# Attention and a two-layer network on one core: keys and queries split at full height, a third form of the products with the values, and neighbouring 64-row products

## The chip, the core and the metric

The kernel runs on one core of a Trainium2 chip. The metric is the time of one launch on the device, in microseconds (us). A core has TensorE (matrix products; PE in the profile, with its weight loads as PEld), VectorE (DVE), ScalarE (ACT), GpSimd (POOL), and SyncE (SP), which issues nearly all transfers here. Each works through its own queue in the order in which the program was written, and they wait for each other on semaphores.

## The reference

```python
batch, n_heads, seq, head_dim = 4, 12, 448, 64
scores = matmul(q, k.T) / sqrt(64)
scores = cap * tanh(scores / cap)              # cap = 30
attn = softmax(scores)                         # over the keys
x = matmul(attn, v)                            # heads side by side: [1792, 768]
h = x @ w_in                                   # [768, 2048]
out = maximum(0.01 * h, h) @ w_out             # [2048, 768]
```

All of it is fp32. A second path, for a cap above 40, stands behind the program's end and isn't taken.

## The kernel before

**Precision.** TensorE has a rounded fp32 form (fp32r here) that takes one pass for a product and a whole one that takes four. Nearly every operand is therefore kept as two parts: `hi`, a copy rounded to fp32r, and `lo`, the remainder. A product is then three passes: hi by hi, hi by lo, lo by hi (line 712). `split` (line 343) makes the parts: a copy on ScalarE or VectorE, then a subtraction on VectorE or GpSimd.

**Attention** goes by pairs of heads, 24 in all (six for each of four batches). Two heads have 896 keys, which are seven tiles of 128: three that belong to the first head (A0 to A2), three to the second (B1 to B3), and one, M, with the last 64 keys of the first head and the first 64 of the second. For a pair, SyncE loads k, q and v; VectorE transposes k and q into `kT` and `qT`, 128 rows of which 64 belong to each head. `stack` (line 449) then builds `kst0` and `kst1`, one for each head: on the head's own 64 rows the hi part of its keys, on the other 64 rows the remainder, so that one pass computes two of the three products. For each head it does a 64-row copy from `kT` and a 64-row subtraction, and a 64 by 64 corner for M into `kb`. Queries are split at 128 rows into `qn` and `qlo` (line 499) and copied, 64 rows at a time, into `qd` and `qz` by an engine or by a transfer. Scores (line 563) take 15 passes a pair and go to PSUM; ScalarE applies tanh (line 575) and exp (line 577) and writes the exponentials `pf`, as keys by queries.

**Products with the values** come in two forms. Pairs 0 to 13 multiply `pf` by the values in whole fp32 (line 591), with a column of ones beside the values, which gives the sums. Pairs 14 to 23 split `pf` into `ph` and `pl` and have the values' hi and lo parts side by side in the weights, so that two passes suffice (lines 434 and 435); the sums are made apart, by adding on VectorE and GpSimd. In both forms head 0's result goes to `po0` and head 1's to `po1`, in different banks of PSUM. For tile M each head uses its own 64 rows alone; head 0 has M last, head 1 has it first or last, and the steps of the two heads are independent of each other.

**The network** runs as 34 units a batch (136 in all): 16 of the first layer (18 passes) and 18 of the second (15 or 18 passes), all at line 687, fed by weights that are split into `w` again for every batch. The result of a unit leaves PSUM through ScalarE (line 722) and VectorE (lines 727 and 736).

**Order.** `Plan` collects steps with a rank and a cost for each engine that could do them. `issue` is a list scheduler: it repeatedly takes the step that can start first by those costs (and by rank among equals), gives it to the engine that would end it first, and writes the instruction there. So the costs and ranks, the table `T` among them, set the order of every queue; SyncE's queue is one of them.

Of the kernel before, what the change touches and what calls it, by code (L numbers as in the profile page):

```python
# [21 lines left out]
    kT=1,  # L22
# [25 lines left out]
    role={'x fixed_vx': -279.8, 'x fixed_v': -32.4, 'pair kraw dma first': -114.6, 'pair kT first': -66.5, 'pair qT first': 8.1, 'pair kst first': 606.4, 'pair kb first': 43.4, 'pair qn first': 404.6, 'pair qlo first': 17.3, 'pair qd first': -209.0, 'pair vx dma first': -44.3, 'pair po first': -143.3, 'pair sums first': 20.8, 'pair rt first': -18.8, 'pair xh first': 234.6, 'pair xl first': -9.0, 'pair vhi first': 5.3, 'pair vlo first': -10.0, 'pair ph first': 8.5, 'pair kraw dma': -80.3, 'pair kT': -351.0, 'pair qraw dma': 216.2, 'pair qT': 158.0, 'pair kst': 58.5, 'pair qn': 715.7, 'pair qlo': 177.0, 'pair vraw dma': 1208.5, 'pair vhi': -301.0, 'pair vlo': -249.7, 'pair ph': -297.4, 'pair pl': 272.8, 'pair po': 65.9, 'pair x': -133.1, 'pair xh': 602.7, 'pair xl': -26.0, 'unit wr dma first': -298.3, 'unit wm first': 89.1, 'unit ws first': -117.6, 'unit scratch dma first': -7.5, 'unit whi first': 97.6, 'unit wlo first': -164.9, 'unit m first': 339.7, 'unit a first': 108.0, 'unit g first': -626.7, 'unit gh first': -746.5, 'unit gl first': -737.6, 'unit acc first': -52.0, 'unit ot first': 88.7, 'unit store dma first': -7.8, 'unit ws dma': 11.8, 'unit whi': 244.8, 'unit wlo': -45.3, 'unit m': 176.3, 'unit a': -38.5, 'unit g': -828.4, 'unit gh': 775.4, 'unit acc': -397.5, 'unit ot': -15.1, 'unit store dma': -171.8, 'unit kraw': 2.4, 'unit qraw': 20.2, 'x cap dma': -698.3, 'x inv': -321.8, 'x ones': -257.6, 'pair qraw dma first': -47.2, 'pair pl first': -5.5, 'pair kb': 777.6, 'pair qd': -145.0, 'pair sc': -71.0, 'pair pf': -287.8, 'pair sums': -262.3, 'pair rt': -218.0, 'pair t': -278.4, 'pair u': -779.0, 'pair uh': -90.3, 'pair ul': 95.2, 'pair ss': -59.8, 'unit gl': -222.5, 'pair vhi.0 zero': 4.1, 'pair vlo.0 zero': -2.7, 'pair ph.0 zero': 2.7, 'pair ph.1 zero': 2.7, 'pair ph.2 zero': 2.7, 'pair ph.3 zero': 2.7, 'pair pl.0 zero': -5.3, 'pair pl.1 zero': -5.3, 'pair pl.2 zero': -5.3, 'pair pl.3 zero': -5.3, 'pair pf first': -131.6, 'pair k0.0 dma zero': 83.1, 'pair q0.0 dma zero': 88.5, 'pair kT0.0 zero': 138.8, 'pair kst0.0 zero': -36.0, 'pair kb.0 zero': 66.5, 'pair qd.0 zero': 8.2, 'pair qlo0.0 zero': -72.2, 'pair q0.1 zero': 10.7, 'pair k0.1 dma zero': 29.5, 'pair q0.1 dma zero': 111.6, 'pair kT0.1 zero': -24.2, 'pair qT0.1 zero': -55.6, 'pair kst1.0 zero': 38.4, 'pair qlo0.1 zero': -12.5, 'pair vx.0 dma zero': -19.5, 'pair sc.0 zero': 3.1, 'pair sc.1 zero': -33.6, 'pair pf.1 zero': 84.1, 'pair pf.2 zero': 587.4, 'pair sc.3 zero': -33.0, 'pair pf.3 zero': -20.3, 'pair po0.0 zero': -1.7, 'pair x.0 zero': 68.1, 'pair po1.0 zero': 28.6, 'pair rt.0 zero': -28.3, 'pair sums.1 zero': -12.7, 'pair x.1 zero': -19.7, 'pair xl.0 zero': -29.3, 'pair sc first': -150.8, 'pair x first': 13.6, 'pair xs': 138.0, 'pair q0.0 zero': 16.0, 'pair qT0.0 zero': -25.2, 'pair qd.1 zero': 79.5, 'pair sc.2 zero': 182.8, 'pair xh.0 zero': 30.1, 'pair pf.0 zero': 4.5, 'pair vhi dma': 26.6, 'pair vx dma': 4.5, 'unit raw first': 36.6},  # L48
    pair=[-1101.8, -433.2, -1118.2, -327.2, 39.0, 378.0, 325.9, 703.0, 321.7, 372.6, 475.8, 149.5, 521.9, 787.1, 552.8, 471.0, 783.4, 77.4, 446.9, 129.6, 408.3, 288.7, 835.1, 264.8],
# [15 lines left out]


class Plan:

    LAT = {"dma": 2.2}

    def __init__(self):
        self.steps = []  # L80
        self.rings = {}
        self.slots = {}
        self.kind, self.phase, self.shift = "x", "", 0.0

    def part(self, kind, phase, shift):

        self.kind, self.phase, self.shift = kind, phase, shift

    def ring(self, tag, n):
# [9 lines left out]
    def add(self, rank, cost, fn, reads=(), writes=(), after=(), lat=0.15, freed=(), port=True):  # L99
        tag = writes[0][0].rstrip("0123456789") if writes else "store"  # L100
        if self.phase == " zero":
            tag = f"{writes[0][0]}.{writes[0][1]}"
        role = self.kind + " " + tag + (" dma" if list(cost) == ["sp"] else "") + self.phase
        rank = hundredths(rank) + hundredths(self.shift) + hundredths(T["role"].get(role, 0.0))
        self.steps.append(dict(role=role, rank=rank, cost={e: hundredths(c) for e, c in cost.items()}, fn=fn, reads=reads,
                               writes=writes, after=list(after), lat=hundredths(lat), freed=freed, port=port))
        return len(self.steps) - 1

# [784 lines left out]
```

## Time and profile before

| | us |
|---|---|
| three runs | 757.99, 758.2, 759.87 |
| median | 758.2 |
| the profiled execution, its whole time | 758.92 |
| its span, first to last instruction | 757.1 |
| TensorE busy in the span | 701.7 |
| VectorE busy | 572.8 |
| ScalarE busy | 512.3 |
| GpSimd busy | 135.7 |

The profile is of one execution, so sums are made against its span of 757.1 us. The mean granted clock of TensorE was 0.977. A row of a matmul runs from the start of a pass to the end of its modelled pipeline, so neighbouring rows overlap: the start-to-start distance is what a pass costs in a dense stream. A whole fp32 product is recorded as two rows. A few rows are missing from the trace.

### The profile page before, as it was taken

The page shows a single profiled execution, that of the slowest core. Times are in us where ns is not written, and L with a number is a line of the kernel's source. Part 1 is how long each engine was busy: PE and PEld are TensorE (multiplying, and loading weights), DVE is VectorE, ACT ScalarE, POOL GpSimd, SP SyncE. Part 2 cuts the span into 40 slices and gives each one's busy share as a digit, 9 for nine tenths or more (in the row PEclk, how much of TensorE's full clock was granted, in tenths as well). Part 3 has the DMA queues.
Part 4 walks back from the last instruction along what each step waited for, and adds up shares of the span by engine and source line. Part 5 has one row for each costly group of instructions (what it writes and reads, how often), then busy time and mean ns, then how long its engine had stood idle before and what let it go on. Part 6 is the DMA issues. An engine that isn't in the chain of part 4 may idle for free.

```text
span 757.1 us, 9414 instructions
## 1 busy us (share of the span) xinstructions
PE 701.7 (93%) x3084; PEld 573.7 (76%) x3084; DVE 572.8 (76%) x856; ACT 512.3 (68%) x778; POOL 135.7 (18%) x132
## 2 busy tenths in 40 slices
PE   7897999999988989899999999999899988999994
PEld 4453578777667777788888888988778876999884
DVE  7888788779878788987799787786986986435443
ACT  6877797788978777885687557666965963434230
POOL 2332320010112111110033211221231420000000
PEclk9998999999999999999999999999999998999997
DMA  6887764976787677635254365443233362333335
GB/s 118 178 198 201 172 169 144 259 229 149 219 226 186 211 206 167 138 94 140 58 140 117 98 137 133 122 113 109 58 97 109 72 144 66 113 105 96 95 92 86
DMA packets 206215, 105.33 MB, mean 139 GB/s; under 512 B 160432, under 2 KB 188720, under 8 KB 206160
## 3 DMA queue, kind: packets, MB, share of 16 engines
q1 hardware_dynamic: 206096, 104.55, 54.1%
q8 instruction: 26, 0.43, 0.3%
q14 instruction: 29, 0.24, 0.1%
q0 software_dynamic: 64, 0.11, 0.1%
HBM read 79.89 MB, written 18.09 MB: 129 GB/s over the span
## 4 chain that ended last, share of the span: by engine, by line
PE 63%; DVE 17%; ACT 9%; DMA 6%; issue 4%; SPq 1%; DVEq 0%; ACTq 0%
PE m L687 48%; PE po L591 6%; PE sc L563 5%; PE po L434 2%; DVE w L238 2%; DMA wr<-in_moe_w_in_dram 2%; PE po L435 2%; ACT pf L575 1%; DVE kst L238 1%; DVE ws L679 1%; DVE wr L676 1%; DVE late L727 1%; DVE pl L238 1%; ACT pf L577 1%; DMA qraw<-in_q_dram 1%
## 5 line engine op out<-in xcount | busy, mean ns | idle before, releaser
L687 PE MATMUL m<-gh,w 128*128 128x448 f32 x768 | 236.1, 375 | 6.7 <-DVE late L736 3.8
L687 PE MATMUL m<-xh,w 128*128 128x448 f32 x768 | 232.7, 374 | 10.2 <-DVE late L727 7.3
L687 PEld LDWEIGHTS m<-xh,w 128*128 128x128 f32 x768 | 145.7, 190 | 30.0 <-DVE late L727 10.5
L687 PEld LDWEIGHTS m<-gh,w 128*128 128x128 f32 x768 | 145.9, 190 | 27.5 <-DVE late L736 4.6
L238 DVE TENSOR_TENSOR w<-ws,w 128x768 fp32r<-128x768 f32 (+1 forms) x124 | 118.5, 963 | 38.4 <-ACT w L231 36.5
L687 PE MATMUL m<-xl,w 128*128 128x448 f32 x384 | 141.9, 370 | 0.2 <-DVE xl L238 0.2
L687 PE MATMUL m<-gl,w 128*128 128x448 f32 x384 | 141.9, 370 | 0.0
L231 ACT CAST w<-ws 128x768 fp32r<-128x768 f32 (+1 forms) x110 | 86.2, 788 | 60.1 <-PE m L687 26.0
L575 ACT ACTIVATE pf<-sc,inv_sb 128x896 f32<-128x896 f32 (+1 forms) x82 | 74.2, 913 | 22.2 <-PE sc L563 11.2
L563 PE MATMUL sc<-qd,kst 128*128 128x448 f32 x192 | 73.4, 402 | 12.2 <-ACT pf L575 8.2
L687 PEld LDWEIGHTS m<-gl,w 128*128 128x128 f32 x384 | 73.1, 190 | 7.1 <-issue 1.1
L687 PEld LDWEIGHTS m<-xl,w 128*128 128x128 f32 x384 | 73.0, 190 | 7.1 <-issue 0.7
L577 ACT ACTIVATE pf<-pf,cap_sb 128x896 f32<-128x896 f32 (+1 forms) x82 | 77.6, 952 | 0.7
L591 PE MATMUL po<-pf,v 128*128 128x448 f32 (+1 forms) x170 | 69.0, 569 | 5.8 <-ACT w L231 2.3
L722 ACT ACTIVATE late<-m 128x448 f32<-128x448 f32 x58 | 31.4, 542 | 53.6 <-PE m L687 50.9
L727 DVE TENSOR_TENSOR late<-m,late 128x448 f32<-128x448 f32 x64 | 39.6, 619 | 28.6 <-ACT late L722 28.3
L563 PEld LDWEIGHTS sc<-qd,kst 128*128 128x128 f32 x192 | 35.9, 188 | 27.7 <-ACT pf L575 14.3
L563 PE MATMUL sc<-qz,kst 128*128 128x448 f32 x144 | 52.7, 366 | 0.2 <-ACT qz L231 0.2
L591 PEld LDWEIGHTS po<-pf,v 128*128 128x128 f32 (+1 forms) x170 | 27.3, 191 | 32.3 <-issue 20.5
L238 POOL TENSOR_TENSOR w<-ws,w 128x640 fp32r<-128x640 f32 (+1 forms) x12 | 21.9, 1830 | 151.4 <-PE m L687 113.0
L736 DVE TENSOR_TENSOR late<-m,late 128x448 f32<-128x448 f32 x48 | 29.4, 617 | 24.5 <-PE m L687 24.1
L238 DVE TENSOR_TENSOR gl<-late,gh 128x448 fp32r<-128x448 f32 x62 | 40.7, 659 | 6.6 <-ACT gh L231 5.9
(110 smaller groups left out, 954.4 us busy)
## 6 DMA issues: line engine op xcount, KB each, us to landing
ws<-scratch SPq DMA_DIRECT2D x66, 384.0 KB, 3.2
wr<-in_moe_w_in_dram SPq DMA_DIRECT2D x16, 768.0 KB, 5.4
ws<-scratch SPq DMA_DIRECT2D x36, 320.0 KB, 2.9
scratch<-ws SPq DMA_DIRECT2D x22, 384.0 KB, 5.5
wr<-in_moe_w_out_dram SPq DMA_DIRECT2D x12, 640.0 KB, 5.0
kraw<-in_k_dram SPq DMA_DIRECT2D x96, 56.0 KB, 2.4
qraw<-in_q_dram SPq DMA_DIRECT2D x94, 56.0 KB, 2.7
wr<-in_moe_w_out_dram SPq DMA_DIRECT2D x6, 768.0 KB, 5.1
```

The lines of the kernel that those rows point to most:

```text
L231: nc.scalar.copy(o, i)
L238: ENG[eng].tensor_tensor(out=o, in0=a, in1=f32(b), op=ALU.subtract)
L434: nc.tensor.matmul(at(f"po{j}", i)[:, 0:S], v_, at("ph", ver)[k, t], start=(m == 0), stop=False)
L435: nc.tensor.matmul(at(f"po{j}", i)[:, 0:S], v_, at("pl", ver)[k, t], start=False, stop=(m == 3))
L563: nc.tensor.matmul(at("sc", ver)[:, t, 0:S], l, r, start=(m == 0), stop=(m == len(mm) - 1))
L575: a = plan.add(r, {"act": ct}, lambda e, sc=sc, pf=pf: nc.scalar.activation(pf(), sc(), AF.Tanh, scale=inv_sb), [("sc", ver), ("inv", 0)], ...
L577: plan.add(r, {"act": ct + 0.03}, lambda e, pf=pf: nc.scalar.activation(pf(), pf(), AF.Exp, scale=cap_sb), (), [("pf", ver)], after=[a])
L591: nc.tensor.matmul(at(f"po{j}", i)[:, 0:S], at("vx", i)[k, c, j:j + 2].rearrange("p o d -> p (o d)"), at("pf", ver)[k, t], start=(n == 0), ...
L687: nc.tensor.matmul(o, l, r, start=(first and m == 0), stop=(last and m == len(mm) - 1))
L722: nc.scalar.mul(at("a", f), ps(), 0.01)
L727: plan.add(rank, {"dve": 0.54}, lambda e: nc.vector.tensor_tensor(out=at("g", f), in0=ps(), in1=at("a", f), op=ALU.max), [("m", m), ("a", ...
L736: op = plan.add(rank, {"dve": 0.54}, lambda e: nc.vector.tensor_tensor(out=acc(), in0=ps(), in1=acc(), op=ALU.add), [("m", m)], [(tag, b)] ...
```

## The change

1. **Third form of the products ("parts").** Pairs 10 to 13 now split `pf` and the values, and do hi by `ph`, hi by `pl` and lo by `ph`. The values' tile has six columns of 64 a chunk: hi of head 0, a fixed one, hi of head 1, lo of head 0, a fixed zero, lo of head 1. So the sums come with the products as in the whole form. Pairs 0 to 9 stay whole.
2. **M's products in one step.** `products` replaces both old loops. The step `shared` does tile M for both heads, one pass of head 0 and one of head 1 in turn.
3. **Keys and queries.** `kT` is copied whole into `kh` and the remainder is written over `kT` (as `kl`). The 64-row halves of both go to `kst0` and `kst1` by `put`: ScalarE, VectorE, GpSimd, or a transfer on SyncE's queue. The corners of `kb` may go by transfer too. `kh` and `kT` have one buffer; `qd`, once a ring of three, is one buffer for each head.
4. **The leak of the first layer** is written into `g`, which becomes a ring of three; the buffer `a` is gone.
5. **Costs, delays and ranks.** The scheduler's costs are new (a pass 0.2045 instead of 0.19), a step's result is taken to be ready 0.10 to 0.20 us after it, with 0.20 more on the way to TensorE, and all ranks in `T` are new. Pair 0 keeps its own code.

```diff
+    np=10,
...
-    LAT = {"dma": 2.2}
+    LAT = {"act": 13, "dve": 12, "pool": 10, "pe": 20}
...
-                lat = max(220, s["lat"]) if eng == "sp" else 0 if eng == "pe" and "pe" in steps[u]["cost"] else s["lat"]
+                to_pe = "pe" in steps[u]["cost"]
+                lat = max(220, s["lat"]) if eng == "sp" else 0 if eng == "pe" and to_pe else self.LAT[eng]
+                lat += 20 if to_pe and eng != "pe" else 0
...
-    ring("qd", T["qd"], [P, S], F32R)
+    ring("kh", 1, [P, S])
+    plan.ring("kl", 1)
+    for j in range(2):
+        ring(f"qd{j}", 1, [P, S], F32R)
...
-    MM = 0.19
-    HALF = {"act": 0.47, "dve": 0.30, "pool": 1.09}
+    MM = 0.2045
+    HALF = {"act": 0.575, "dve": 0.40, "pool": 1.1}
+    MOVE = dict(HALF, sp=0.48)
...
+    way = lambda i: "whole" if i < T["np"] else "parts" if i < SUMS else "sums"
+    def products(i, r0, where):
...
+        def passes(j, c, k, ver, t):
+            p = lambda tag: at(tag, ver)[k, t]
+            if how == "whole":
+                return [(flat(at("vx", i)[k, c, j:j + 2]), p("pf"))]
+            if how == "parts":
+                hi, lo = (flat(at("vz", i)[k, c, n + j:n + j + 2]) for n in (0, 3))
+                return [(hi, p("ph")), (hi, p("pl")), (lo, p("ph"))]
+            both = flat(at("vs", i)[k, c, 2 * j:2 * j + 2])
+            return [(both, p("ph")), (both, p("pl"))]
...
+        def shared(e, g=g, t=t):
+            both = [passes(j, PM[j], half[j], NG * i + g, t) for j in range(2)]
+            end = len(both[0]) - 1
+            for n in range(end + 1):
+                for j in range(2):
+                    l, r = both[j][n]
+                    nc.tensor.matmul(at(f"po{j}", i)[:, 0:S], l, r, start=(mid and j == 1 and n == 0), stop=(n == end and not (mid and j == 1)))
...
-        for j in range(2):
-            stack(r0 + T["pk"], j, i, ("kT", i), HALF, LO)
+        plan.add(r, {"act": 0.47, "dve": 0.31}, lambda e: copy(e, f32r(at("kh", i)), at("kT", i)), [("kT", i)], [("kh", i)])
+        plan.add(r, WHOLE, lambda e: ENG[e].tensor_tensor(out=f32r(at("kT", i)), in0=at("kT", i), in1=at("kh", i), op=ALU.subtract),
+                 [("kT", i), ("kh", i)], [("kl", i)])
...
+        def put(rank, j_in, dst, src, reads, writes, cost=MOVE):
+            def fn(e):
+                if e == "sp":
+                    nc.sync.dma_start(out=f32(dst()), in_=f32(src()))
+                else:
+                    copy(e, dst(), f32(src()), zeros[half[j_in]])
...
+            put(r, j, lambda j=j, h=h, c=c: at(f"kst{j}", i)[h, c], lambda h=h: at("kh", i)[h], [("kh", i)], [(f"kst{j}", i)])
+            put(r, j, lambda j=j, o=o, c=c: at(f"kst{j}", i)[o, c], lambda h=h: at("kT", i)[h], [("kl", i)], [(f"kst{j}", i)])
```

How this moves instructions is seen in the order of the queues. The first place is TensorE's queue at the products of one of the last ten pairs, before: `po0` and `po1` are the two heads' results, `ph_3` and `pl_3` the exponentials of tile M, `ph_2` and `pl_2` those of tiles B2 and B3, `m` a unit of the network.

```order
L563 MATMUL sc_0_96<-qz1_0_83,kst1_1_90 128x448
L434 MATMUL po0_0_88<-ph_3_103,v_0_second_1937 128x448
L435 MATMUL po0_0_88<-pl_3_107,v_0_second_1937 128x448
L687 MATMUL m_1_159<-gh_0_142,w_2_140 128x448
...
L687 MATMUL m_1_159<-gh_2_144,w_2_140 128x448
L434 MATMUL po1_0_91<-ph_2_102,v_0_second_1937 128x448
...
L435 MATMUL po1_0_91<-pl_2_106,v_0_second_1937 128x448
L434 MATMUL po1_0_91<-ph_3_103,v_0_second_1937 128x448
L435 MATMUL po1_0_91<-pl_3_107,v_0_second_1937 128x448
```

And a pair of the last ten in the changed program:

```order
L481 MATMUL po1_0_91<-ph_2_102,v_1_second_1625 128x448
L481 MATMUL po1_0_91<-pl_2_106,v_1_second_1625 128x448
L471 MATMUL po0_0_88<-ph_3_103,v_1_second_1625 128x448
L471 MATMUL po1_0_91<-ph_3_103,v_1_second_1625 128x448
L471 MATMUL po0_0_88<-pl_3_107,v_1_second_1625 128x448
L471 MATMUL po1_0_91<-pl_3_107,v_1_second_1625 128x448
L630 MATMUL sc_1_97<-qd0_0_79,kst0_0_86 128x448
```

Head 0's two passes with M stood apart from head 1's, with a unit and tiles B2 and B3 between; now the four stand together and alternate.

The second place is TensorE's queue at one of pairs 10 to 13, in the changed program only (before, these were rows of line 591 with `pf`).

```order
L481 MATMUL po0_0_88<-ph_1_101,v_1_second_1625 128x448
L481 MATMUL po0_0_88<-pl_1_105,v_1_second_1625 128x448
L481 MATMUL po0_0_88<-ph_1_101,v_1_second_1625 128x448
L471 MATMUL po0_0_88<-ph_1_101,v_1_second_1625 128x448
L471 MATMUL po1_0_91<-ph_1_101,v_1_second_1625 128x448
L471 MATMUL po0_0_88<-pl_1_105,v_1_second_1625 128x448
L471 MATMUL po1_0_91<-pl_1_105,v_1_second_1625 128x448
L471 MATMUL po0_0_88<-ph_1_101,v_1_second_1625 128x448
L471 MATMUL po1_0_91<-ph_1_101,v_1_second_1625 128x448
```

A product is three passes with split exponentials instead of one whole one, and M's six passes alternate between the heads.

The third place is SyncE's queue at one of the last ten pairs, in the changed program: `ws` are weights, `qd`, `qz` and `kst1` the operands of the scores, `kh` and `kT` the two parts of the keys.

```order
L714 DMA ws_1_137<-scratch25_185 128x768
L556 DMA qd0_0_79<-qn_0_77 64x448
L556 DMA qd1_0_80<-qn_0_77 64x448
L556 DMA qz0_0_82<-qlo_0_81 64x448
L556 DMA qz1_0_83<-qlo_0_81 64x448
L714 DMA ws_0_136<-scratch24_184 128x768
L556 DMA kst1_0_89<-kh_0_78 64x448
L556 DMA kst1_0_89<-kT_0_75 64x448
L376 DMA qraw_0_73<-in_q_dram 32x14x32 x4
```

Before, `qd` and `qz` could stand between the weight loads; the halves of `kst1` are new there.

More of the change, by code (lines that the diff above doesn't have):

```diff
@@ L284, in softcap_attention_mlp @@
         alias(f"acc{e}", [late[:, e]])
-    alias("g", [late[:, NE], late[:, NE + 1]])
-    alias("a", [late[:, NE + 2]])
+    alias("g", [late[:, NE + n] for n in range(3)])
     alias("ot", [late[:, NE + 3].rearrange("p (s d) -> p s d", d=32)])
@@ L441, in summed_values, with pv @@
                 out=at("xs", i)[r], in0=at(f"po{j}", i)[r, 0:S], in1=at("xs", i)[r], op=ALU.add), [(f"po{j}", i)], [("xs", i)], after=[a], freed=narrowed, port=False)
+    def products(i, r0, where):
+        half = [slice(0, 64), slice(64, P)]
+        how = way(i)
+        flat = lambda ap: ap.rearrange("p o d -> p (o d)")
+        def passes(j, c, k, ver, t):
[7 more added lines that the diff above has]
+            return [(both, p("ph")), (both, p("pl"))]
+        per, of_m = {"whole": (4 * 0.188, 1.45), "parts": (3 * MM, 1.25), "sums": (2 * MM, 0.95)}[how]
+        vals = [("vx", i)] if how == "whole" else [("vhi", i), ("vlo", i)]
+        exps = lambda ver: [("pf", ver)] if how == "whole" else [("ph", ver), ("pl", ver)]
+        g, t = where["M", 0]
+        mid = g == 1
+        def shared(e, g=g, t=t):
[5 more added lines that the diff above has]
+                    nc.tensor.matmul(at(f"po{j}", i)[:, 0:S], l, r, start=(mid and j == 1 and n == 0), stop=(n == end and not (mid and j == 1)))
+        last = []
+        for j in range(2):
+            for m, (wc, c) in enumerate(PV[j]):
+                g_, t_ = where[wc]
+                def pv(e, j=j, m=m, c=c, t=t_, ver=NG * i + g_):
+                    both = passes(j, c, slice(0, P), ver, t)
+                    for n, (l, r) in enumerate(both):
+                        nc.tensor.matmul(at(f"po{j}", i)[:, 0:S], l, r, start=(m == 0 and n == 0 and not (mid and j == 1)),
+                                         stop=(mid and j == 1 and m == 2 and n == len(both) - 1))
+                last = [plan.add(r0 + T["pp"] + 4 * j, {"pe": per}, pv, vals + exps(NG * i + g_), [(f"po{j}", i)], after=last)]
+            if j == (0 if mid else 1):
+                last = [plan.add(r0 + T["pp"] + 3 + j, {"pe": of_m}, shared, vals + exps(NG * i + g), [("po0", i), ("po1", i)], after=last)]
@@ L513, in low @@
-            def low(e, j=j):
-                r = half[j]
-                if e == "sp":
-                    nc.sync.dma_start(out=f32(at(f"qz{j}", i)[r]), in_=f32(at("qlo", i)[r]))
-                else:
-                    copy(e, at(f"qz{j}", i)[r], f32(at("qlo", i)[r]), zeros[r])
-            plan.add(r0 + T["pk"] + T["kq"] + j, dict(HALF, sp=0.48), low, [("qlo", i)], [(f"qz{j}", i)])
+                put(r + j, j, lambda j=j, o=o: at(f"qd{j}", i)[o], lambda h=h: at("qn", i)[h], [("qn", i)], [(f"qd{j}", i)])
@@ L522, in plan_pair @@
+            put(r + j, j, lambda j=j, h=h: at(f"qz{j}", i)[h], lambda h=h: at("qlo", i)[h], [("qlo", i)], [(f"qz{j}", i)])
     def plan_pair(i):
-        plan.part("pair", " zero" if i == 0 else " first" if i < NP else "", T["pair"][i])
+        plan.part("pair", " zero" if i == 0 else " first" if i < NP else "", i)
         r0 = 10.0 * i
@@ L531, in plan_pair @@
         where = {wc: (g, t) for g, grp in enumerate(groups) for t, wc in enumerate(grp)}
-        if i < SUMS:
+        how = way(i)
+        if how == "whole":
             plan.add(r0 - T["al"] + 1, {"sp": 1.4}, lambda e: load_vx(i, at("vx", i)), [("fixed_vx", 0)], [("vx", i)], lat=2.5)
@@ L691, in plan_unit @@
     def plan_unit(m, rank):
-        plan.part("unit", " first" if m < NU else "", T["unit"][m])
+        plan.part("unit", " first" if m < NU else "", m)
         b, n = divmod(m, NU)
```

139 lines of the change are left out of this document (67 added, 72 removed).

## The prediction

> **What bounds the kernel now.** I read the page's busy times first, then the table of stretches, then TensorE's waits, and last its timeline around the products with the values.
>
> ```profile
> PE 701.7 (93%) x3084; PEld 573.7 (76%) x3084; DVE 572.8 (76%) x856; ACT 512.3 (68%) x778; POOL 135.7 (18%) x132
> PE 63%; DVE 17%; ACT 9%; DMA 6%; issue 4%; SPq 1%; DVEq 0%; ACTq 0%
> ```
> ```profile
> 200.00:300.00 100.00, 91.18 (x383) 70.61 (x382) 79.79 (x117) 77.57 (x114) 18.08 (x20) 0.98 0.75 198
> 560.00:640.00 80.00, 76.61 (x344) 65.13 (x345) 59.38 (x88) 49.38 (x74) 17.13 (x11) 0.96 0.40 100
> ```
>
> TensorE is busy for 701.7 of 757.1 us and holds 63% of the chain that ended last. From 200 to 300 us it is busy 91%, VectorE 80% and ScalarE 78%; from 560 to 640 us 96%, the others 74 and 62%. So a microsecond of TensorE work is worth nearly a microsecond, unless another engine takes its place. What TensorE loses by waiting is in its waits (us in total, times, longest):
>
> ```profile
> PE m L687 <- DVE late L727: 9.5, 7, 3.8
> PE sc L563 <- ACT pf L575: 8.2, 11, 3.0
> PE m L687 <- DVE late L736: 5.7, 5, 2.0
> PE po L591 <- DVE x L619: 5.3, 2, 3.3
> PE sc L563 <- ACT late L575: 4.0, 3, 3.6
> PE po L591 <- ACT w L231: 2.3, 1, 2.3
> PE po L591 <- DMA v<-in_v_dram: 0.6, 1, 0.6
> ```
>
> That is 35.6 us, of which 14.5 us were ended by ScalarE (8.2 + 4.0 + 2.3) and 0.6 us by a transfer.
>
> **The 64-row products, term one.** The shared ("M") tile of a pair is used twice, once for each head, on 64 rows each. In the last ten pairs (lines 434 and 435) it is two passes a head. Here is one head alone, between passes on 128 rows (start, us busy):
>
> ```profile
> 394.63 0.37 PE L563 MATMUL sc<-qz,kst 128*128 128x448 f32 x1
> 394.92 0.47 PE L434 MATMUL po<-ph,v_second 64*128 64x448 f32 x1
> 395.23 0.36 PE L435 MATMUL po<-pl,v_second 64*128 64x448 f32 x1
> 395.52 0.47 PE L687 MATMUL m<-gh,w 128*128 128x448 f32 x1
> 395.84 0.37 PE L687 MATMUL m<-gl,w 128*128 128x448 f32 x1
> ```
>
> From 394.63 to 395.84 are 1.21 us for two ordinary passes and the two 64-row ones. Ordinary passes lie 0.20 us apart where nothing changes (346.66 follows 346.46 below), so the two 64-row passes cost 0.80 us, twice what two full ones would. Where both heads happened to be neighbours, it looks like this:
>
> ```profile
> 346.46 0.36 PE L434 MATMUL po<-ph,v_second 128*128 128x448 f32 x1
> 346.66 0.37 PE L435 MATMUL po<-pl,v_second 128*128 128x448 f32 x1
> 346.95 0.47 PE L434 MATMUL po<-ph,v_second 64*128 64x448 f32 x2
> 347.27 0.37 PE L435 MATMUL po<-pl,v_second 64*128 64x448 f32 x2
> 347.56 0.47 PE L687 MATMUL m<-gh,w 128*128 128x448 f32 x1
> 347.87 0.36 PE L687 MATMUL m<-gl,w 128*128 128x448 f32 x1
> ```
>
> Two 64-row passes of one group take 0.47 us together, as one does alone, so the two heads run at the same time. From 346.66 to 347.87 is again 1.21 us, now with four 64-row passes: 0.80 us for both heads instead of 1.60. How often that already happens is told by busy time against count:
>
> ```profile
> L434 PE MATMUL po<-ph,v_second 64*128 64x448 f32 x20 | 9.4, 494 | 0.0
> L591 PE MATMUL po<-pf,v 64*128 64x448 f32 x44 | 14.3, 588 | 0.0
> ```
>
> At line 434, 20 x 0.494 = 9.9 us of rows cover 9.4 us: one overlap of 0.47, so one pair of ten. At line 591, 44 x 0.588 = 25.9 us of rows cover 14.3 us: most pairs are neighbours there, and the order names the three that are not (pairs 1, 6 and 10). The change puts both heads into one step, alternating, in every pair. In the last ten pairs this takes 9 x 0.80 = **7.2 us** off TensorE. For the whole-precision form one head alone reads:
>
> ```profile
> 93.76 1.86 PE L591 MATMUL po<-pf,v 128*128 128x448 f32 x4
> 95.55 0.47 PE L687 MATMUL m<-xh,w 128*128 128x448 f32 x1
> 95.86 0.36 PE L687 MATMUL m<-xl,w 128*128 128x448 f32 x1
> ```
>
> From 93.76 to 95.55 are one 128-row product (0.75, below) and one of 64 rows: 1.04, with 0.11 that the next pass loses (0.31 instead of 0.20) 1.15 us. Three pairs would save 3.4 us; pair 1 lies in the first 40 us, where TensorE waits anyway, so I take two: **2.3 us**.
>
> **The third form, term two.** Pairs 10 to 13 change from whole products to three rounded passes (hi by hi, hi by rest, rest by hi).
>
> ```profile
> 219.35 2.42 PE L591 MATMUL po<-pf,v 128*128 128x448 f32 x6
> L591 PE MATMUL po<-pf,v x170: 536/539/1116, 13.9 to 295.5; 128*128 128x448 f32 x126, 64*128 64x448 f32 x44
> ```
>
> Six rows are three products: 2.42 less the last row's own 0.54 is 1.88 for five starts, 0.376 a row, 0.75 a product. Three passes at 0.203 are 0.61. A pair has six such products (6 x 0.14 = 0.86) and the two 64-row ones: 1.15 together now, and by the rows above 0.80 for two rounds plus 0.31 for the third, 1.11. Saved 0.90 a pair, **3.6 us** for four; pair 10's being apart is in the term before.
>
> Its price is splitting the exponentials and values. One pair gains three hi casts of 896 columns and one of 448 and two of the values, and the remainders behind them:
>
> ```profile
> L231 ACT CAST ph<-pf 128x896 fp32r<-128x896 f32 x29 | 27.1, 943 | 0.3
> L231 ACT CAST ph<-pf 128x448 fp32r<-128x448 f32 x10 | 5.7, 566 | 0.2
> L231 ACT CAST v_second<-vraw 128x256 fp32r<-128x256 f32 x19 | 7.2, 402 | 3.7 <-PE po L435 3.6
> L238 DVE TENSOR_TENSOR pl<-pf,ph 128x896 fp32r<-128x896 f32 x29 | 34.1, 1177 | 1.8 <-ACT ph L231 1.4
> L238 DVE TENSOR_TENSOR kst<-kT,kst 64x448 fp32r<-64x448 f32 x35 | 25.9, 739 | 1.8 <-ACT kst L231 0.8
> L238 DVE TENSOR_TENSOR xl<-x,xh 128x448 fp32r<-128x448 f32 x21 | 14.1, 671 | 4.3 <-ACT xh L231 4.1
> L231 ACT CAST kst<-kT 64x448 fp32r<-64x448 f32 x25 | 14.1, 563 | 4.7 <-DVE kT L386 4.3
> ```
>
> On ScalarE that is 3 x 0.94 + 0.57 + 2 x 0.40 = 4.2 us a pair. On VectorE ten remainders more (10 x 1.18 = 11.8 us).
>
> **Keys and queries.** Each head's key was cast and subtracted at 64 rows: two casts and two remainders a pair. Now it is one cast and one remainder at 128 rows, since a row count costs nothing (0.563 at 64 rows, 0.566 at 128), and four moves. The order has 33 fewer 64-row remainders on VectorE (-33 x 0.739 = -24.4 us) and 13 full ones (+13 x 0.671 = 8.7). With the remainders above, and about 7 us net from casts and weights that the planner places on it, VectorE comes out +3 us. ScalarE gains 18 full key casts (+10), the 14 exponential and 9 value casts (+15) and loses moves and small casts: +20 us on 512. GpSimd comes out within 4 us. The queues get 63 transfers more: 39 of key halves, 14 of key corners, 14 of queries, 4 of values, less 8 half loads of values.
>
> Cost on the path: TensorE waited 14.5 us for ScalarE's 512, so 20 more should show as 20/512 of it, 0.6 us; bounds are nothing and 8.4 us (half of the 4 x 4.2, if ScalarE sets the pace of those four pairs). The transfers: 58 such moves stand in the kernel now, and TensorE's waits on a transfer are 0.6 us, so I take 0.6; the upper bound is the third rival.
>
> **The order** is new throughout. That moves the 35.6 us of waits, either way; its bounds are half of the long ones gone, or as much new. I take 0. What else a wait costs is in the granted clock (stretch, length, TensorE busy; then the other engines, and the clock as the first of the last three numbers):
>
> ```profile
> 211.00:213.40 2.40, 0.38 (x3) 0.35 (x3) 2.37 (x5) 2.35 (x4) 0.00 (x0) 0.99 0.63 113
> 213.40:216.70 3.30, 3.30 (x11) 2.92 (x10) 3.27 (x7) 2.60 (x4) 0.00 (x0) 0.50 0.94 230
> ```
>
> A stall of 2 us is followed by 3.3 us at half clock, in which half the work of the stretch, some 1.6 us, is lost besides. The Trainium skill ("TensorE: Matmul & The Clock Gate", section "HAM oscillation — how this bites in real kernels") puts the fall of the clock behind idle gaps of more than about 3.4 us. The trace does not agree: it fell behind a stall of 2.0 us. By the rule the first rival below would bring 736 us, with one such stretch fewer (two of the five stalls are that long, half of them go); by the row it brings 733.
>
> **Sum.** The profiled span is 757.1 - 7.2 - 2.3 - 3.6 + 0.6 + 0.6 = 745.2. That execution took 758.9 in all, 0.7 over the median of 758.2, so 1.1 us lie around the span when measured against the median: **746 us**.
>
> **Rivals.**
>
> *The order also removes stalls.* For: the new costs lie closer to the trace (a pass 0.2045, where the row gives 0.203 and the old number was 0.19), and the pairs stand more evenly between the units: by the order on TensorE, 33 unit passes stood between its 165th and its 195th score product (eleven and thirteen pairs' worth), and now 105 do. Against: nothing shows which waits go. If half of the five longest above (3.8, 3.6, 3.3, 3.0, 2.3: 16 us) go with three half-clock stretches of 1.6, 13 us more: 733.
>
> *ScalarE sets the pace of pairs 10 to 13.* For: it is busy 78% from 200 to 300 us, and 4.2 us a pair come on top. Against: the ten later pairs split in the same way and TensorE is still 96% busy beside them. Price 8.4 instead of 0.6: 754.
>
> *Key halves come late through SP's queue* (slower). SP issues in order, and its queue stands still behind weight loads:
>
> ```profile
> SPq L658 <- DVE w L238: 173.0, 74, 7.0
> qd<-qn SPq DMA_DIRECT2D x34, 112.0 KB, 2.4
> ```
>
> A key half that came from an engine now waits behind a load that waits for a weight buffer (2.3 us on average), and takes 2.4 us to land; scores, ScalarE's tanh and the products queue behind it. In some 20 pairs it happens at least once. From 0.65 us a pair it eats the 13 us; at 1 us a pair, with the half clock behind every other one left out, it is 746 + 20 = 766. Against: query halves take that way 58 times today, with 0.6 us of waits.
>
> *Alternation does not overlap as neighbours do*, so terms one vanish: 746 + 9.5 = 755.5. Against: both forms show the overlap (x2 rows above).
>
> **Chances.** Forecast 0.50 (own range 740 to 751), order 0.18, ScalarE 0.15, SP's queue 0.12, no overlap 0.05. A measurement tells 0.3% (2.3 us) from no change. Faster (under 755.9): 0.49 + 0.18 + 0.11 + 0.02 = 0.80; same: 0.08, from the second and fourth rival's edges; slower: 0.12, the third and little else. The range for 8 in 10 is 733 to 757: it takes in the second rival, leaves half of the first and the third out.
>
> **What would show it.** The 64-row rows all as x2, with busy time half of count times mean; in the last ten pairs two rounds of 0.3 us each. Rows of three passes in pairs 10 to 13 at 0.20 apart. TensorE's busy time some 12 us lower with its waits about where they were. Wrong would be: TensorE waits on transfers to the key tile by more than 5 us, or waits on ScalarE in the stretch of pairs 10 to 13 that alone come near the old 14.5 for the whole kernel. Waits on VectorE's line of the maximum (9.5 us) being gone would speak for the first rival.

## The result, and the profile after

| | before | after |
|---|---|---|
| median (4 runs each) | 759.04 us (757.99 to 762.29) | 740.64 us (738.75 to 742.96) |
| ratio, with its 95% interval | | 0.9752 [0.9706, 0.9797] |
| the profiled execution, whole time and span | 758.92, 757.1 us | 739.27, 737.4 us |

The change makes the kernel 2.5% faster: 18.4 us by the medians, 19.7 us between the two profiled spans. The forecast was 12 us.

The page after, its busy times and the shares of the chain of work that ended last:

```profile
PE 685.2 (93%) x3116; PEld 573.5 (78%) x3116; DVE 570.0 (77%) x860; ACT 527.7 (72%) x802; POOL 138.1 (19%) x135
PE 42%; ACT 16%; DVE 16%; DMA 16%; issue 5%; SPq 3%; POOL 1%; DVEq 0%; ACTq 0%; POOLq 0%
```

TensorE's busy time fell by 16.5 us, ScalarE's rose by 15.4. TensorE holds 42% of the chain of work that ended last, where it held 63%: that chain now runs through a mixture of engines. The same two stretches (TensorE, its weight loads, VectorE, ScalarE, GpSimd, then granted clock, DMA share, GB/s):

```profile
200.00:300.00 100.00, 93.04 (x426) 77.00 (x425) 90.26 (x130) 89.42 (x135) 28.61 (x27) 0.98 0.83 207
560.00:640.00 80.00, 79.82 (x391) 71.99 (x391) 61.57 (x94) 50.75 (x77) 6.63 (x5) 1.00 0.44 112
```

From 560 to 640 us TensorE has next to no gap left (busy 79.82 of 80 us; 76.61 before), and it gets through 391 passes instead of 344. From 200 to 300 us VectorE and ScalarE are at 90 and 89%, where they were at 80 and 78. TensorE's waits after (us in total, times, longest):

```profile
PE m L743 <- DVE late L783: 6.6, 7, 1.4
PE m L743 <- DVE late L792: 6.1, 4, 2.4
PE sc L630 <- ACT pf L642: 4.4, 8, 1.1
PE sc L630 <- ACT qz L234: 3.4, 1, 3.4
PE sc L630 <- DMA qz<-qlo: 3.4, 2, 2.1
```

All of TensorE's waits sum to 40.9 us against 44.9 before. The line of the maximum (L783) went from 9.5 to 6.6, its longest wait from 3.8 to 1.4 us. No wait is put down to the transfers of key halves; two are to a transfer of queries, 3.4 us.

**A ledger of the span.** For this kernel and for the experiments I split each profiled span into three: TensorE idle (the 3.1 us before its first row and all gaps between its rows up to the last one), the half clock (half of the time recorded at a granted clock of 0.5, after the first warm stretch and before the end), and what is left, which is TensorE's work at full clock with about 10 us behind its last row. What is left is rough. Ends are modelled, some rows are missing, and a gap that lies in a half-clock stretch is counted one and a half times (0.3 us of such gaps in the kernel after, 5.1 in the one with a cost 1% lower). Kernels that issue the same passes in much the same way differ by up to 8 us in it (681.8 to 689.7 in the table of the experiments). The profiled execution of "M joined" was a slow one, 782.85 us at a granted clock of 0.838, so that kernel has no ledger, and the ratios leave such executions out.

| us | span | idle | half clock | left: work |
|---|---|---|---|---|
| before | 757.1 | 45.6 | 13.7 | 697.9 |
| after | 737.4 | 42.2 | 8.5 | 686.6 |
| difference | -19.7 | -3.4 | -5.2 | -11.2 |

By the ledger some 11 of the 20 us are work that TensorE no longer has, and some 9 are stalls and the half clock behind them (eight times 3.4 us at half clock before, five times after). With that scatter the split between the two is no more than a first indication.

### The profile page after: what moved, and what is told of

It reads as the page before. It is cut to its first block, busy times and chain, and to the rows that moved or that the text cites. A ratio compares the mean times of both kernels' runs of the same rounds, so it can differ in the third digit from the quotient of the medians.

```text
span 737.4 us, 9647 instructions
## 1 busy us (share of the span) xinstructions
PE 685.2 (93%) x3116; PEld 573.5 (78%) x3116; DVE 570.0 (77%) x860; ACT 527.7 (72%) x802; POOL 138.1 (19%) x135
## 4 chain that ended last, share of the span: by engine, by line
PE 42%; ACT 16%; DVE 16%; DMA 16%; issue 5%; SPq 3%; POOL 1%; DVEq 0%; ACTq 0%; POOLq 0%
PE m L743 33%; PE po L481 4%; PE sc L630 4%; DMA scratch<-ws 4%; DMA wr<-in_moe_w_out_dram 3%; DMA ws<-scratch 3%; ACT pf L644 3%; DVE w L241 3%; ACT pf L642 3%; DMA wr<-in_moe_w_in_dram 2%; ACT w L234 2%; DVE ws L735 2%; SPq L376 2%; DVE wr L732 1%; DVE pl L241 1%
## 5 line engine op out<-in xcount | busy, mean ns | idle before, releaser
L743 PE MATMUL m<-gh,w 128*128 128x448 f32 x768 | 231.7, 372 | 14.7 <-DVE late L792 5.0
L743 PE MATMUL m<-xh,w 128*128 128x448 f32 x768 | 228.7, 369 | 5.4 <-DVE late L783 3.1
L241 DVE TENSOR_TENSOR w<-ws,w 128x768 fp32r<-128x768 f32 (+1 forms) x131 | 124.2, 952 | 36.9 <-ACT w L234 32.7
L234 ACT CAST w<-ws 128x768 fp32r<-128x768 f32 (+1 forms) x112 | 88.0, 789 | 64.0 <-DMA ws<-scratch 35.1
L630 PE MATMUL sc<-qd,kst 128*128 128x448 f32 x192 | 75.3, 412 | 7.0 <-ACT pf L642 4.4
L778 ACT ACTIVATE late<-m 128x448 f32<-128x448 f32 x59 | 31.9, 541 | 44.9 <-PE m L743 44.6
L783 DVE TENSOR_TENSOR late<-m,late 128x448 f32<-128x448 f32 x64 | 39.5, 618 | 26.0 <-ACT late L778 25.4
L630 PEld LDWEIGHTS sc<-qd,kst 128*128 128x128 f32 x192 | 37.7, 196 | 24.1 <-ACT pf L642 10.9
L241 DVE TENSOR_TENSOR pl<-pf,ph 128x896 fp32r<-128x896 f32 (+1 forms) x48 | 49.6, 1039 | 3.7 <-ACT ph L234 3.3
L241 DVE TENSOR_TENSOR gl<-late,gh 128x448 fp32r<-128x448 f32 x62 | 42.9, 694 | 6.7 <-ACT gh L234 6.2
L234 ACT CAST ph<-pf 128x896 fp32r<-128x896 f32 (+1 forms) x53 | 44.0, 840 | 0.5
L241 POOL TENSOR_TENSOR v_second<-vraw,v_second 128x256 fp32r<-128x256 f32 x28 | 27.6, 1002 | 69.0 <-ACT v_second L234 68.6
```

The costliest lines, as they stand in the source:

```text
L234: nc.scalar.copy(o, i)
L241: ENG[eng].tensor_tensor(out=o, in0=a, in1=f32(b), op=ALU.subtract)
L630: nc.tensor.matmul(at("sc", ver)[:, t, 0:S], l, r, start=(m == 0), stop=(m == len(mm) - 1))
L743: nc.tensor.matmul(o, l, r, start=(first and m == 0), stop=(last and m == len(mm) - 1))
L778: nc.scalar.mul(at("g", f), ps(), 0.01)
L783: plan.add(rank, {"dve": 0.54}, lambda e: nc.vector.tensor_tensor(out=at("g", f), in0=ps(), in1=at("g", f), op=ALU.max), [("m", m)], [("g" ...
```

## The experiments

Every ratio is to the kernel before, run on the same chip beside it; its median there was 759.04 to 760.57 us. Most intervals reach 0.003 to 0.005 to either side, so two ratios are told apart from about 0.006 (4.4 us) on. The ledger is that of each profiled execution.

| kernel | median us | ratio [95%] | span | idle | half clock | work |
|---|---|---|---|---|---|---|
| after | 740.64 | 0.9752 [0.9706, 0.9797] | 737.4 | 42.2 | 8.5 | 686.6 |
| M joined in the old kernel | 750.84 | 0.9892 [0.9858, 0.9926] | | | | |
| after, M's passes apart | 746.7 | 0.9822 [0.9784, 0.9859] | 744.8 | 43.2 | 6.8 | 694.7 |
| after, M's passes grouped | 741.93 | 0.977 [0.9735, 0.9806] | 740.5 | 43.2 | 11.9 | 685.3 |
| after, pairs 10 to 13 whole | 756.88 | 0.9967 [0.9939, 0.9996] | 754.6 | 53.1 | 11.9 | 689.6 |
| after, old key splitting | 772.22 | 1.0172 [1.0119, 1.0224] | 771.9 | 64.8 | 18.8 | 688.4 |
| new steps, old costs and ranks | 753.02 | 0.991 [0.9878, 0.9941] | 752.3 | 50.7 | 17.1 | 684.5 |
| old steps, new costs and ranks | 769.51 | 1.0133 [1.0076, 1.0191] | 767.9 | 53.3 | 20.5 | 694.1 |
| after, one cost 1% lower | 763.99 | 1.0079 [1.0055, 1.0103] | 759.6 | 57.3 | 20.5 | 681.8 |
| before, one cost 1% lower | 760.65 | 1.0013 [0.9991, 1.0036] | 755.7 | 46.1 | 11.9 | 697.7 |
| after, key moves on ScalarE | 745.28 | 0.9809 [0.9774, 0.9844] | 742.6 | 47.2 | 8.5 | 686.9 |
| after, two passes in pairs 10 to 13 | 742.19 | 0.9773 [0.9731, 0.9815] | 740.2 | 48.0 | 10.2 | 681.9 |
| after, casts twice in pairs 10 to 13 | 745.56 | 0.9816 [0.9787, 0.9846] | 744.6 | 49.8 | 5.1 | 689.7 |

Where an edit alters the steps that the scheduler sees, it makes a new order for all queues, and the time holds the edit and the new order together. Where only what a step issues is altered, every queue keeps its order: this is said with each.

### M joined in the old kernel

The kernel before, with `products` and its step `shared` in place of the two old loops, nothing else. The order is made anew with the old costs and ranks.

```diff
-        for j in range(2):
-            last = []
...
-                last = [plan.add(r0 + T["pp"] + 4 * j, {"pe": 2 * MM}, pv, ...)]
+        products(i, r0, where)
...
```

> The kernel before, with one part of the change: tile M of both heads in one step, the passes alternating; costs, ranks, keys and the two forms as before (the scheduler runs again, so the order moves a little). My theory (64-row passes of the two heads run at the same time): TensorE does 9 x 0.80 + 2 to 3 x 1.15 = 9.5 to 10.7 us less, so about 749 us against 759. Rival (most of the change's gain came from the new costs and ranks, which take stalls away): the joined step alone is worth 3 us or less, 756 or more.

Measured: 750.84 us, ratio 0.9892, which is 8.2 us off the kernel before, give or take 2.6. Term one was forecast at 9.5 us. That the passes overlap is in the trace: the rows of the last ten pairs at the joined step cover half of count times mean (20 x 0.473 is 9.5 us over 4.8), where before one pair of ten overlapped.

```profile
L465 PE MATMUL po<-ph,v_second 64*128 64x448 f32 x20 | 4.8, 473 | 0.0
```

The order is a new one here too, so the 8.2 us hold whatever that is worth; the next edits keep the order.

### After, M's passes apart and M's passes grouped

Two edits inside the step `shared`, in the order of the changed kernel. Apart: in the last ten pairs, head 1's two passes with tile B3 go between head 0's passes with M and head 1's. They are issued later than planned, when their exponentials can already have been overwritten, and this kernel's result is wrong; the passes are the same in number and size.

```diff
+            if how == "sums":
+                for j in range(2):
+                    for n in range(end + 1):
+                        l, r = both[j][n]
+                        nc.tensor.matmul(at(f"po{j}", i)[:, 0:S], l, r, start=False, stop=(n == end))
+                    if j == 0:
+                        held[i]()
+                return
...
```

Grouped: the four (or six) passes stay together, but no longer alternate.

```diff
-            for n in range(end + 1):
-                for j in range(2):
+            for j in range(2):
+                for n in range(end + 1):
```

> The changed kernel, order of all queues kept except that in the last ten pairs tile B3's two passes stand between head 0's two passes with M and head 1's two. My theory: each pair pays the change of rows twice, and the two heads no longer overlap: 10 x 0.80 = 8 us more, 748.6. Rival (TensorE's work there is hidden by other engines' waits, so it was the order that gained): 742 or less.

> The changed kernel, order of all queues kept except that in the joint step both passes of head 0 stand first and then those of head 1, not in turn (14 pairs with two or three passes a head). If TensorE starts a pass of the other 64 rows ahead of one that waits for its own rows, as the neighbours of the kernel before showed (two starts 0.007 us apart, then two more 0.31 us later), nothing changes: 740 to 741. If passes start strictly in the order of the program, the second pass of head 0 waits, then head 1 starts beside it, and its second pass needs a round of its own: 14 x 0.3 = 4.2 us more, 745.

TensorE's timeline at M in one of the last ten pairs (start, us busy). In the changed kernel:

```profile
603.72 0.36 PE L743 MATMUL m<-gh,w 128*128 128x448 f32 x1
604.00 0.47 PE L471 MATMUL po<-ph,v_second 64*128 64x448 f32 x2
604.31 0.37 PE L471 MATMUL po<-pl,v_second 64*128 64x448 f32 x2
604.61 0.47 PE L743 MATMUL m<-xh,w 128*128 128x448 f32 x1
```

With the passes apart (L472 are M's, L496 tile B3's):

```profile
609.78 0.37 PE L758 MATMUL m<-gh,w 128*128 128x448 f32 x1
610.08 0.47 PE L472 MATMUL po<-ph,v_second 64*128 64x448 f32 x1
610.38 0.36 PE L472 MATMUL po<-pl,v_second 64*128 64x448 f32 x1
610.68 0.47 PE L496 MATMUL po<-ph,v_second 128*128 128x448 f32 x1
610.99 0.37 PE L496 MATMUL po<-pl,v_second 128*128 128x448 f32 x1
611.29 0.47 PE L472 MATMUL po<-ph,v_second 64*128 64x448 f32 x1
611.60 0.36 PE L472 MATMUL po<-pl,v_second 64*128 64x448 f32 x1
611.88 0.47 PE L758 MATMUL m<-xh,w 128*128 128x448 f32 x1
```

From the pass before M to the pass behind it are 0.89 us in the first and 2.10 in the second, of which two ordinary passes of 0.20 are tile B3's. Apart costs 0.81 us a pair more; the prediction had 0.80. Over ten pairs that is 8.1 us. The ledger's work rises by as much (686.6 to 694.7), though that is no more than its scatter; the rows are the firmer figure. Of it 5 to 6 us show in the time: 6.1 by the medians, 5.3 by the ratios, both near the edge of what can be told apart.

Grouped can't be told from after (741.93 us, ratio 0.977 against 0.9752). Its M step, in the program's order and then as recorded:

```
L471 MATMUL po0_0_88<-ph_3_103,v_0_second_1498 128x448
L471 MATMUL po0_0_88<-pl_3_107,v_0_second_1498 128x448
L471 MATMUL po1_0_91<-ph_3_103,v_0_second_1498 128x448
L471 MATMUL po1_0_91<-pl_3_107,v_0_second_1498 128x448
```

```profile
606.89 0.37 PE L743 MATMUL m<-gh,w 128*128 128x448 f32 x1
607.19 0.47 PE L471 MATMUL po<-ph,v_second 64*128 64x448 f32 x2
607.50 0.37 PE L471 MATMUL po<-pl,v_second 64*128 64x448 f32 x2
607.80 0.47 PE L743 MATMUL m<-xh,w 128*128 128x448 f32 x1
```

The third pass of the program, head 1's with `ph`, is recorded beside the first and ahead of the second. What is worth the 0.8 us is that the two heads stand together, not that they alternate.

### After, pairs 10 to 13 whole, and after with the old key splitting

Two parts undone, each with a new order.

```diff
-    np=10,
+    np=14,
```

> The changed kernel with the third form undone: pairs 10 to 13 whole again, everything else as changed (the scheduler runs again with ranks that were set for the third form). My theory: TensorE does 4 x 0.9 = 3.6 us more and ScalarE some 17 us less; 744 us against 740.6. Rival (the splitting's 17 us on ScalarE and 17 on VectorE were paid on the path, so the third form was a loss that other parts covered): 740 or less. Second rival (the old M products there were the gain): no difference from my theory here.

```diff
-        plan.add(r, {"act": 0.47, "dve": 0.31}, lambda e: copy(e, f32r(at("kh", i)), at("kT", i)), [("kT", i)], [("kh", i)])
...
+        for j in range(2):
+            stack(r0 + T["pk"], j, i, ("kT", i), HALF, LO)
```

> The changed kernel with keys and queries split as before (two 64-row copies and two 64-row remainders a pair, written straight into the score operands; moves of keys by transfer gone); the scheduler runs again. My theory: the key part is worth little by itself, since VectorE and ScalarE have room; the difference is that of a newly made order, within 10 us of 740.6, mostly above: 741 to 751. Rival (full-height splitting is what took stalls away, 33 remainders of 0.74 us off VectorE): 752 or more, with TensorE's waits on VectorE several us up in the first 320 us.

Measured 756.88 and 772.22 us: 16 and 32 us slower than after, far beyond what my theories gave for the parts (744, and 741 to 751). By the ledger little of it is work: 3.0 and 1.8 us, both within its scatter, against 10.9 and 22.6 us of idle and 3.4 and 10.3 of half clock. In the first kernel stalls lie where nothing was edited. Here it is from 560 to 640 us, where all its pairs have the form that they have in after:

```profile
560.00:640.00 80.00, 73.79 (x343) 65.23 (x343) 56.71 (x85) 48.46 (x71) 10.06 (x7) 0.96 0.41 106
```

TensorE is idle for 6.2 of these 80 us, in after for 0.2. The second kernel's longest waits:

```profile
PE m L732 <- DVE late L772: 15.7, 12, 4.7
PE po L481 <- DVE x L664: 9.2, 6, 3.7
```

These waits are put down to VectorE's work on the output of the units and on `x`, and none of weight to the keys. But VectorE works through one queue, and the rival named just this: 752 us or more, with TensorE's waits on VectorE up in the first 320 us. They are, from 14.5 to 25.5 us there. So this run doesn't tell the 64-row remainders on VectorE from its new order. What speaks for the order is that other edits with a new order stall in the same way without touching the keys: 16 us for the first kernel here, and 23 for a nudge of one cost below.

### Costs and ranks apart from the steps

The new steps with the old costs, delays and ranks (the smaller costs and all of `T` are set back too; the kinds of steps that are new have no rank of their own among the old ones):

```diff
-    MM = 0.2045
-    HALF = {"act": 0.575, "dve": 0.40, "pool": 1.1}
+    MM = 0.19
+    HALF = {"act": 0.47, "dve": 0.30, "pool": 1.09}
...
-                lat = max(220, s["lat"]) if eng == "sp" else 0 if eng == "pe" and to_pe else self.LAT[eng]
-                lat += 20 if to_pe and eng != "pe" else 0
+                lat = max(220, s["lat"]) if eng == "sp" else 0 if eng == "pe" and to_pe else s["lat"]
...
```

> The changed kernel with the scheduler's old costs, delays and ranks (new kinds of steps get rank offset nothing); all parts of the change in the instructions themselves stay. My theory (11 us of the gain is TensorE work that no order changes, the rest is the order): 748 to 756, TensorE's idle and half-clock loss up by 8 us or more against the changed kernel. Rival (the order gave nothing, the new steps gave all): 741 to 744.

The old steps with the new costs, delays and ranks is the same edit the other way round, on the kernel before:

> The kernel before with the new costs, delays and ranks alone; instructions as before but for where they stand and which engine does them. My theory: ranks are fitted to their own set of steps, so they are not a gain for another: 755 to 768. Rival (new costs are truer, and that takes stalls away in any program): 752 or less, 7 us or more under the kernel before.

Measured 753.02 us, within the 748 to 756 expected, and 769.51 us, just above the 755 to 768. With ratios, the four corners are:

| | old costs and ranks | new ones |
|---|---|---|
| old steps | 1 | 1.0133 |
| new steps | 0.991 | 0.9752 |

The new numbers make the old steps 10 us slower and the new steps 12 us faster. The work of TensorE falls in both columns, by 13.4 us (697.9 to 684.5) and by 7.5 (694.1 to 686.6), which the ledger's scatter doesn't tell apart. With the old ranks 13.4 us of work go, and 5.1 us of idle and 3.4 of half clock come in. One place where they come in is the stretch of pairs 10 to 13, here in the kernel with the new steps and the old ranks:

```profile
200.00:300.00 100.00, 86.75 (x383) 72.73 (x382) 88.41 (x126) 91.84 (x138) 29.40 (x27) 0.91 0.73 190
```

ScalarE is busy for 92% there, TensorE for 87% at a clock of 0.91, and it gets through 383 passes where after does 426. TensorE's waits in that stretch:

```profile
PE m L742 <- ACT w L233: 4.1, 2, 2.8
PE po L480 <- DVE pl L240: 3.2, 1, 3.2
PE m L742 <- DVE w L240: 2.3, 3, 1.4
PE po L480 <- POOL pl L240: 1.8, 1, 1.8
PE sc L629 <- ACT pf L641: 1.3, 4, 0.5
```

They sum to 13.2 us, of which 5.9 are put down to ScalarE; in after they are 6.5 and 0.8. Over the whole kernel the longest wait in total is the one on tanh:

```profile
PE sc L629 <- ACT pf L641: 10.8, 12, 4.4
```

### One cost, 1% lower

If an order is fitted to one set of steps and numbers, a nudge that means nothing should upset it.

```diff
-    MM = 0.2045
+    MM = 0.2025
```

> The changed kernel with one scheduler cost nudged by 1% (a pass 0.2025 instead of 0.2045), so that the order is made anew and nothing else differs: the size of the accident in a new order. My theory: ranks are fitted to one order, and any new order is 3 to 15 us longer by stalls: 744 to 756. Rival (the order is sturdy, so that runs with one part undone measure that part): 739 to 743.

Measured 763.99 us, 23 us more than after and beyond the 744 to 756 of my theory, with the same steps. (TensorE's passes are the same; some steps go to another engine, so that ScalarE has 786 instructions instead of 802 and VectorE 875 instead of 860.) Three of TensorE's waits, which were 6.6, 4.4 and 1.2 us in after:

```profile
PE m L743 <- DVE late L783: 14.7, 9, 4.3
PE sc L630 <- ACT pf L642: 9.7, 9, 2.7
...
PE po L481 <- DVE x L675: 5.9, 4, 2.7
```

The same on the kernel before:

```diff
-    MM = 0.19
+    MM = 0.188
```

> The kernel before with one scheduler cost nudged by 1% (a pass 0.188 instead of 0.19), so that the order is made anew and nothing else differs. My theory (its ranks are fitted to one order as those of the changed kernel are): 765 to 785, so that the change between two unfitted orders (against the changed kernel nudged, 764) is again about 10 us of TensorE work. Rival (the old order is sturdy, and the change made the kernel easier to upset): 756 to 763.

760.65 us, ratio 1.0013: no change, so my theory that every order here is that touchy fell. The old one isn't, by this one nudge; the new one is. It is a new order all the same: VectorE has 834 instructions instead of 856, and the two heads' passes with M happen to be neighbours in five of the last ten pairs instead of one (20 x 0.467 is 9.3 us over 7.3):

```profile
L434 PE MATMUL po<-ph,v_second 64*128 64x448 f32 x20 | 7.3, 467 | 0.9 <-ACT ph L231 0.9
```

### Key moves on ScalarE

After, in its order; the 39 key halves that went by transfer are copied by ScalarE, at the place of the order where SyncE's issue stood.

```diff
-                if e == "sp":
+                if e == "sp" and writes[0][0][:3] == "kst":
+                    copy("act", dst(), f32(src()), zeros[half[j_in]])
+                elif e == "sp":
                     nc.sync.dma_start(out=f32(dst()), in_=f32(src()))
```

> The changed kernel, order of all queues kept, but the 39 moves of key halves that went by transfer are copies on ScalarE, in the same places (39 x 0.56 = 22 us more on ScalarE, 39 transfers fewer on SyncE's queue). My theory: the transfers were hidden and ScalarE is not, so it gets a little longer: 742 to 750. Rival (third rival of the prediction: key halves come late behind weight loads): 738 or less.

Measured 745.28 us, some 4 us more than after, at the edge of what can be told and within the 742 to 750 expected. ScalarE's busy time is up by 19.5 us:

```profile
PE 685.9 (92%) x3116; PEld 572.2 (77%) x3116; DVE 572.0 (77%) x860; ACT 547.2 (74%) x841; POOL 134.9 (18%) x135
```

Taking the halves off SyncE's queue gains nothing that outweighs what it puts on ScalarE. In after the halves take 3.0 and 3.2 us from issue to landing (issues, KB each, us):

```profile
kst<-kh SPq DMA_DIRECT2D x20, 112.0 KB, 3.2
kst<-kT SPq DMA_DIRECT2D x19, 112.0 KB, 3.0
```

That is more than the 2.4 of a query half before, but no wait of TensorE's is put down to them. Together this says that they were not late there.

### What paces pairs 10 to 13

Two edits in the order of after. First, the third pass of the new form (lo by `ph`) is left out, and with it that small part of the product:

```diff
-                return [(hi, p("ph")), (hi, p("pl")), (lo, p("ph"))]
+                return [(hi, p("ph")), (hi, p("pl"))]
```

> The changed kernel, order of all queues kept, but pairs 10 to 13 leave out the third pass (rest of the values by hi of the exponentials), 24 passes on 128 rows and 8 on 64. The products lose their small part. My theory: TensorE's passes in that stretch are on the path, 24 x 0.203 + 4 x 0.2 = 5.7 us less: 735. Rival (ScalarE and VectorE set the pace there, at 89 to 90% busy from 200 to 300 us): 739 or more.

Second, the hi cast of the exponentials is done twice in these pairs, by whichever engine has it:

```diff
+        def whole(e):
+            copy(e, o_hi(), src())
+            if again:
+                copy(e, o_hi(), src())
+
...
-            split(r + T["ps"], ph, pl, pf, n * S, [("pf", ver)], ("ph", ver), ("pl", ver))
+            split(r + T["ps"], ph, pl, pf, n * S, [("pf", ver)], ("ph", ver), ("pl", ver), again=how == "parts")
```

> The changed kernel, order of all queues kept, but in pairs 10 to 13 each hi copy of the exponentials is done twice (14 copies more on ScalarE, 2 on VectorE, 12 to 13 us in all). My theory: most of it lies beside TensorE's work: 742 to 746. Rival (second rival of the prediction: ScalarE sets the pace of those pairs): 750 or more.

The stretch with a pass fewer, and then with the cast twice:

```profile
200.00:300.00 100.00, 87.98 (x387) 69.98 (x387) 88.61 (x126) 87.24 (x132) 29.76 (x27) 0.98 0.81 204
```

```profile
200.00:300.00 100.00, 87.52 (x397) 70.23 (x397) 86.62 (x123) 94.05 (x142) 27.96 (x27) 1.00 0.80 199
```

Leaving out 32 passes (24 of 0.20 us, and four rounds of M's, each two passes in 0.20: 5.6 us) gains nothing that can be told, 742.19 us where 735 was expected: TensorE is 88 instead of 93 us busy and idles for the rest, and the ledger has 4.7 us less work and 5.8 more idle. The casts add 10.3 us to ScalarE (538.0 against 527.7) and some 5 us to the time (745.56), give or take 4. TensorE's waits from 200 to 300 us, 6.5 in after, become 11.6 with a pass fewer, of which 10.4 are put down to VectorE, and 12.4 with the casts twice, of which 8.6 to VectorE and 3.8 to ScalarE. So in these pairs and in this order TensorE has slack, and VectorE and ScalarE between them have little.

## Why the prediction was right, and which term was not

The forecast of 746 us had the sign and came within 6 us of the time. Of the mechanism it had the 64-row passes; it had the change of order at nothing, which was wrong, and the third form worth more than the runs show. Term by term:

- **64-row products, 9.5 us: right.** Joining M alone, in a new order, took 8.2 us off the old kernel; taking M apart in ten pairs, in the kept order, put 8.1 us on TensorE's rows (7.2 were forecast for nine pairs) and 5 to 6 on the time. The rows behave as told: busy time at line 471 is half of count times mean.

```profile
L471 PE MATMUL po<-ph,v_second 64*128 64x448 f32 x36 | 8.1, 444 | 0.0
L471 PE MATMUL po<-pf,v 64*128 64x448 f32 x28 | 7.2, 588 | 0.0
```

  36 x 0.444 = 16.0 us of rows cover 8.1; 28 x 0.588 = 16.5 cover 7.2. The fourth rival (no overlap, 755.5) falls, and passes that stand apart cost the 0.8 us a pair that the prediction took from its rows.

- **Third form, 3.6 us: right as rows, wrong as time.** Its three passes are there, 0.20 us apart (at pair 10 they start at 241.94, 242.15 and 242.35), and M's third round costs 0.20 where I had taken 0.31:

```profile
243.25 0.47 PE L471 MATMUL po<-ph,v_second 64*128 64x448 f32 x2
243.56 0.36 PE L471 MATMUL po<-pl,v_second 64*128 64x448 f32 x2
243.76 0.37 PE L471 MATMUL po<-ph,v_second 64*128 64x448 f32 x2
```

  Going back to the whole form put 3.0 us on the ledger's work, which its scatter doesn't tell from nothing. The step "a microsecond of TensorE work is worth nearly a microsecond" failed from 200 to 300 us: 5.6 us of passes fewer gained nothing there. It was read from a stretch in which VectorE and ScalarE were at 80 and 78%, and the change itself brought them to 90 and 89.

- **ScalarE, 0.6 us: probably too small.** Its busy time rose by 15.4 us (20 forecast). What that cost in the changed kernel no run shows by itself. The two edits that put more on it, 10.3 and 19.5 us, cost about 5 and 4 us of time, so roughly 0.2 to 0.5 of what is added, both at the edge of what can be told; scaling the old waits by 20/512 gives far less than that. (Those waits were 17.5 us with the small rows; the 14.5 were of the three longest.) The second rival's 754 comes near the 753.02 us with the old ranks, but its mechanism is only part of that: with ScalarE at 92% from 200 to 300 us, 5.9 of TensorE's 13.2 us of waits there are put down to it. In the changed kernel they are 0.8 there, and 14.8 over the whole kernel, so the rival falls, and so does the sign of being wrong that was set for it.

- **Transfers, 0.6 us: too small by 2 us.** TensorE waits 3.4 us for them (0.6 before), twice for queries, never for a key half. The third rival (766) falls.

- **The order, taken as 0: this is the term that was mis-sized.** The new costs and ranks measure 12 us with the new steps: 0.991 to 0.9752, ±4; part of that can be that the new kinds of steps have no rank among the old ones. The first rival named the right things (stalls that go, half-clock stretches with them) and had 13 us for them. The ledger of the changed kernel has 8.5 us less idle and 8.6 less half clock than that of the new steps with the old numbers. Against the kernel before it has only 3.4 and 5.2 less, and the line of the maximum, whose 9.5 us of waits were to be gone by this rival's sign, still has 6.6.

In a chain of kernels, each with an order of its own: M joined -8.2; the third form, the keys and the rest of the steps besides, with the old numbers, +1.4 ±3.5; the new numbers -12.0. That makes the 18.8 us of the ratio. Forecast were -9.5, -2.4 and 0. So 746 came near 741 with an error of 12 us in one direction and about 5 in the other, and that they partly cancel was luck.

What stays open is what the third form and the key splitting are each worth under an order fitted to them, since taking either away makes another order, and a percent of one cost already makes one that is 23 us slower. Open is also why the new order is so much more easily upset than the old, and how much of the 32 us without the key splitting is VectorE's 64-row remainders. Whether some other set of ranks would serve the old steps as well was not tried: the 12 us belong to these numbers with these steps.

## What to carry to other kernels

Products on half the rows are worth pairing: find two that use different halves and let them stand next to each other. Price work that is taken off the leading engine by the busy shares of the others in that very stretch, and after the change, not before: here, where two others came to 90%, 5.6 us of it were worth nothing that could be told. And where a list scheduler makes the order, a rank table is fitted to one set of steps: an ablation that makes the order anew measures the new order, so keep the order and alter what a step issues, or nudge a cost by a percent first, to learn how large that noise is (23 us in the changed kernel, more than the whole change is worth, and nothing in the one before).

## What the runs showed of the hardware

Two 64-row passes that use different halves were recorded as starting together (each round 0.3 us for both) even where a pass of the same half stood between them in the program. The Trainium skill ("TensorE: Matmul & The Clock Gate", section "The mechanism") says that matmuls start and end strictly in the program's order. The trace of the grouped kernel does not agree as to starts: the third pass of the program is recorded beside the first, at 607.19, and the second at 607.50.

The cost of a change between 128 and 64 rows is in the rows of M in the changed kernel: the pass before M takes 0.28 us to the next start instead of 0.20 (603.72 to 604.00), and the last round before the next pass on 128 rows 0.30 (604.31 to 604.61). From one round of 64 rows to the next it was 0.31 us there; in the three rounds of pair 10 it was 0.31, then 0.20.
